# The sixth tile's attention visit moved ahead of its blocks, and five instead of three of its block pairs by seven products

## The chip, the cores and the metric

The kernel runs on one core of one Trainium2 chip. The metric is device time in microseconds (us) of one execution; less is better. The three runs of the kernel before have a median of 218.5 us (218.24 to 219.65).

## What is computed

A linear-attention recurrence with decay (retention) over 4 sequences of 768 steps, 8 heads of 64, and behind it a bilinear feed-forward layer on its 3072 output rows of 512:

```
for t in range(S):
    state = gamma * state + einsum('bhd,bhe->bhde', k[:, :, t], v[:, :, t])
    y[:, :, t] = scale * einsum('bhd,bhde->bhe', q[:, :, t], state)
x = y.transpose(0, 2, 1, 3).reshape(B * S, H * D)      # 3072 x 512
out = ((x @ w_a) * (x @ w_b)) @ w_out                  # 512 -> 1536 -> 512
```

Inputs and output are float32; the kernel multiplies in bfloat16.

## The kernel before

**Attention.** The rows are cut into 24 slots of 128 (6 a sequence). For two slots at a time a *visit*, the function `turn(new, old)`, issues a block of small 64x64 matmuls: for the old pair the part of its output that comes from the state, in two halves (L375), for the new pair the chunk states (st, L300) and the scores (at, L330), and for the old pair the part within the chunk (L387). Between the two halves of the state's part stands a fence: a tiny ACT copy `mark` (L352) waits for PE's first half, and PE's second half waits for `mark`. What follows a visit is done later by other engines: DVE adds the chunk states up (sums, L314) and masks the scores (aT, L336), ACT casts the states (gst, L207) and casts the finished outputs y into the feed-forward input xt (L402, `leave`). The ACT pieces wait in a list, `later`, from which `catch_up(n)` issues the next n; the masks wait in `unmasked`, from which `mask_now` issues them. POOL scales k and q (kqb, L248) and casts v (vb, L209); the transposes kqT are DMAs on SP's queue.

**Feed-forward.** The 24 slots make 8 tiles (J = 0 to 7) of 4, 2, 2, 2, 2, 4, 4 and 4 slots, so tiles 5, 6 and 7 have 512 rows. For each tile PE runs twelve a blocks (`ffn_a`, L614, four 128x512 matmuls) and twelve g blocks (`ffn_g`, L626), one for each 128 of the 1536 inner columns. ACT casts a to asb (L618) and DVE multiplies, ht = g * asb (L629). The output product ht @ w_out (`ffn_fast`, L786) is done by Winograd's form of Strassen's scheme: seven products instead of eight, with sums of ht (hsum, L684) as left and sums of w_out (wt_bf) as right operands. Its running sums stand in PSUM banks R1, R2 and R5: PE writes R1, ACT snaps it (snap, L798) or DVE adds a snap to it into the output tile osb (L801), and PE goes on writing to the same bank.

**Pairs by seven products.** In tiles 6 and 7 some pairs of a blocks are done in the same scheme (`seven_a`, L726: fourteen 128x256 matmuls instead of eight of 128x512). `SEVEN` gives the range of pairs f: 1 to 3 in tile 6, 1 to 5 in tile 7. The left operands are the weights wa_bf and sums of them, ta, which POOL makes (`combine_a(f)`, L704, four instructions a pair); the right ones are the tile's xt and sums of it, xs, which DVE makes (`combine_x(J)`, L695, four instructions). Their PSUM banks (`own_banks`) are those that a visit uses for y, at and st. ACT snaps them (L743, L746, L753, L765) and DVE adds them up (L740). The sums hsum of such pairs are made on POOL (`sums_of`), those of plain blocks on DVE.

**The order.** Each engine executes its instructions in the order in which the program issues them (`seq` chains them). The main loop runs the tiles one after the other, blocks and then output; a table `ahead` says what else is issued at which place: (6, 8) is ahead of block 8 of tile 6, (5, "late", 0) and (5, "sums", 0) are places in the first output product of tile 5, (6, "o", 0) is ahead of the output of tile 6. `gate` makes POOL's next instruction wait for DVE's last one. In tile 6 before: a(0), a(1), three pairs by seven products, the visit of slots 22 and 20, blocks 8 to 11 plain, the last visit (of 22 alone), the output.

Of the kernel before, what the change touches and what calls it, by code (L numbers as in the profile page):

```python
# [9 lines left out]
F32 = mybir.dt.float32  # L10
# [5 lines left out]
TILES = [4, 2, 2, 2, 2, 4, 4, 4]  # L16
FAST = (1, 2, 3, 4, 5, 6, 7)
ASIDE = ((1, 0), (2, 0), (3, 0), (4, 0), (5, 0), (6, 0), (6, 1), (7, 0))
SEVEN = {6: (1, 4), 7: (1, 6)}
SPARE = {(J, ft) for J in (2, 3, 4) for ft in range(1, 6 if J == 4 else 10, 2)}  # L20
PAIRS = 3

# [5 lines left out]
def kernel(  # L28
# [11 lines left out]
    P = 128  # L40
# [26 lines left out]
    psff = ctx.enter_context(tc.tile_pool(name="psff", bufs=3, space=bass.MemoryType.PSUM))  # L67
# [10 lines left out]
    def seq(bi):  # L78
        ins = bi.ins
        if gates and ins.engine == mybir.EngineType.Pool:  # L80
            tc.add_manual_dep(ins, gates.pop(), after, reason="behind VectorE's sums")
        prev = last.get(ins.engine)
        if prev is not None:
            tc.add_manual_dep(ins, prev.name, nosync, reason="program order")
        last[ins.engine] = ins
        return bi
# [101 lines left out]
    def late_tables():  # L188
        seq(nc.gpsimd.memset(mask, 1.0))
        for c in range(2):  # L190
            mc = mask[64 * c : 64 * c + 64]
            seq(nc.gpsimd.affine_select(out=mc, in_=mc, compare_op=ALU.is_ge, fill=0.0, base=0,
                                        pattern=[[0, 1], [1, 2], [2, D // 2]],
                                        channel_multiplier=-1))
        return positions([[P, NCH], [0, 1]], 1), positions([[P, NCH], [0, 1]], 2, True)

    late = late_tables()
# [32 lines left out]
    xt, where = {}, {}  # L230
# [48 lines left out]
    def catch_up(n=100):  # L279
        for fn in later[:n]:  # L280
            fn()
        del later[:n]
# [5 lines left out]
    sums = {}  # L288
# [103 lines left out]
    def new_xt(J):  # L392
        xt[J] = xtp.tile([P, 2, KT, 2, P], BF16, tag="xt", name="xt")

    def leave(o, c, apart):
        J, i = where[o]
        if i == 0 and c == 0:
            new_xt(J)
        dst = xt[J][:, i // 2].rearrange("p k par (s c m) -> p c s (k par) m", s=2, c=2)[:, c]
        src = ys[o][c].rearrange("p s k (par m) -> p s (k par) m", par=2)  # L400
        if apart is None:
            seq(nc.scalar.copy(dst, src))  # L402
        else:
            on, off = slice(4 - 4 * c, 8 - 4 * c), slice(4 * c, 4 * c + 4)
            part = tra.tile([P, 2, 2, D], F32, tag="kq"[c] + "T2", name="part", bufs=2)
            seq(nc.scalar.copy(part, apart[c][:, :, 2 - 2 * c : 4 - 2 * c]))
            part = part.rearrange("p s k (par m) -> p s (k par) m", par=2)
            for s in range(2):
                seq(nc.vector.tensor_tensor(dst[:, s, on], src[:, s, on], part[:, s], op=ALU.add))
                seq(nc.vector.tensor_copy(dst[:, s, off], src[:, s, off]))  # L410
# [161 lines left out]
    def xcols(J, kt, c0, c1):  # L572
        W2 = 2 * P
        x = xt[J][:, c0 // W2 : (c1 + W2 - 1) // W2, kt].rearrange("p u par m -> p u (par m)")
        return x if c1 - c0 > W2 else x[:, 0, c0 % W2 : c0 % W2 + c1 - c0]
# [18 lines left out]
    def parts(J, ft, c0, c1):  # L594

        if J == 0 and 2 <= ft < 10:
            return [(c0, (c0 + c1) // 2), ((c0 + c1) // 2, c1)]
        return [(c0, c1)]

    def ff_bank(J, ft, c, name):  # L600

        if (J, ft) in SPARE:
            return psat.tile([P, 4 * P], F32, tag=f"y{c}", name=name)
        return psff.tile([P, 4 * P], F32, tag="ff", name=name)

    def ffn_a(J, ft, c0=0, c1=None):
        c1 = TILES[J] * P if c1 is None else c1
        if J not in ht:
            ht[J] = htp.tile([P, NFT, 4 * P], BF16, tag="ht", name="ht")
        fs = slice(ft * P, (ft + 1) * P)  # L610
        a = ff_bank(J, ft, 0, "a")[:, : c1 - c0]
        for kt in range(KT):
            for b0, b1 in parts(J, ft, c0, c1):
                seq(nc.tensor.matmul(a[:, b0 - c0 : b1 - c0], wa_bf[:, kt, fs], xcols(J, kt, b0, b1),  # L614
                                     start=(kt == 0 and b0 == c0), stop=(kt == KT - 1 and b1 == c1),
                                     skip_group_check=True))
        asb = asbs[J, ft, c0] = asbp.tile([P, 4 * P], BF16, tag="asb", name="asb")[:, : c1 - c0]
        seq(nc.scalar.copy(asb, a))  # L618
# [69 lines left out]
    def combine_x(J):  # L688
        xs[J] = raw.tile([P, 4, 2, 2 * P], BF16, tag="q" * (J == 6) + "k" * (J == 7) + "f", name="xs")
        a11, a12, a21, a22 = (xt[J][:, u, 2 * c : 2 * c + 2].rearrange("p k par m -> p k (par m)")  # L690
                              for u in range(2) for c in range(2))
        s1, s2, s3, s4 = (xs[J][:, i] for i in range(4))
        for dst, x, y, op in ((s1, a21, a22, ALU.add), (s2, s1, a11, ALU.subtract),
                              (s4, a12, s2, ALU.subtract), (s3, a11, a21, ALU.subtract)):
            seq(nc.vector.tensor_tensor(dst, x, y, op=op))  # L695
# [12 lines left out]
    def own_banks(J):  # L708
        at = psat.tile([P, 2, 4 * P], F32, tag="at", name="a")
        st = psst.tile([P, 4 * P], F32, tag="st", name="a")  # L710
        y = [psat.tile([P, 4 * P], F32, tag=f"y{c}", name="a") for c in range(2)]
        banks[J] = [[y[f % 2][:, : 2 * P], st[:, : 2 * P], at[:, f % 2, : 2 * P]] for f in range(2)]
# [16 lines left out]
    def seven_a(J, f):  # L729

        W2 = 2 * P
        if J not in banks:
            own_banks(J)
        R1, R2, R5 = banks[J][f % 2]
        snap = raw.tile([P, 4, W2], F32, tag="vf", name="snap")
        even, odd = (asbp.tile([P, 4 * P], BF16, tag="asb", name="asb") for _ in range(2))
        asbs[J, 2 * f, 0], asbs[J, 2 * f + 1, 0] = even, odd

        def plus(dst, R, x):
            seq(nc.vector.tensor_tensor(dst, R, x, op=ALU.add))  # L740

        part_a(J, f, R1, 1, True)
        seq(nc.scalar.copy(snap[:, 0], R1))  # L743
        part_a(J, f, R2, 2, True)
        part_a(J, f, R5, 5, True)
        seq(nc.scalar.copy(snap[:, 2], R5))  # L746
        for fn in behind[:1]:
            fn()
        plus(even[:, :W2], R2, snap[:, 0])
        catch_up(2)  # L750
        ffn_g(J, 2 * f - 1)
        part_a(J, f, R1, 6, False)
        seq(nc.scalar.copy(snap[:, 1], R1))  # L753
        for fn in behind[1:]:
            fn()
        behind.clear()
        part_a(J, f, R5, 3, False)
        plus(odd[:, :W2], R5, snap[:, 1])
        catch_up(2)
        ffn_g(J, 2 * f - 2)  # L760
        part_a(J, f, R1, 7, False)

        def last_of():
            part_a(J, f, R1, 4, False)
            seq(nc.scalar.copy(even[:, W2:], R1))  # L765

        behind.extend((lambda: plus(odd[:, W2:], R1, snap[:, 2]), last_of))
# [145 lines left out]
    W2 = 2 * P  # L913
# [46 lines left out]
    for j in range(NO):  # L960
# [14 lines left out]
        (5, 0): [(casts, 20, "kq")], (5, 2): [(casts, 21, "kq"), (casts, 20, "v"), (casts, 21, "v")],  # L975
        (5, 3): [(turn, 16, None)], (5, 5): [(casts, 22, "kq")],
        (5, 6): [(casts, 23, "kq")], (5, 8): [(turn, 18, 16)],
        (5, "late", 0): [(gate,), (combine_a, 1), (casts, 22, "v"), (casts, 23, "v"), (combine_a, 2), (combine_a, 3)],
        (5, "sums", 0): [(turn, 20, 18)],
        (6, 8): [(turn, 22, 20)], (6, "o", 0): [(turn, None, 22)], (6, "late", 0): [(gate,), (combine_a, 4), (combine_a, 5)],  # L980
    }
    early = {3: [(0, 0, 2)], 4: [(1, 0, 2)], 5: [(2, 0, 2)], 6: [(3, 0, 2)],
             7: [(0, 2, 4)], 8: [(1, 2, 4)], 9: [(2, 2, 4)], 10: [(3, 2, 4)]}
# [4 lines left out]
    def visit(*at):  # L988
        for fn, *what in ahead.pop(at, ()):
            fn(*what)  # L990
# [8 lines left out]

    def blocks_seven(J):  # L1000
        f0, f1 = SEVEN[J]
        combine_x(J)
        store()
        for ft in range(2 * f0):
            ffn_a(J, ft)
        for f in range(f0, f1):
            seven_a(J, f)
            sums_of(J, f - 1)
            mask_now(1)
        seven_end(J, f1 - 1)  # L1010
        sums_of(J, f1 - 1)
        return 2 * f1
# [17 lines left out]
    def blocks(J):  # L1030
        done = blocks_seven(J) if J in SEVEN else 0
        for ft in range(done, NFT):
# [4 lines left out]
            if J in FAST:  # L1037
                for which, f0, f1 in adds_of(J, ft):
                    if J not in SEVEN or f0 >= 4:
                        add(J, which, f0, f1)  # L1040
# [3 lines left out]
    for J in range(len(TILES)):  # L1044
        if J > 1:
            blocks(J)
        for i in range(TILES[J]):
# [6 lines left out]
            elif i % 2 == 0:  # L1054
                if not J in SEVEN:
                    for which, f0, f1 in adds_of(J, NFT):
# [33 lines left out]
```

## Time and profile before

| | |
|---|---|
| median of three runs | 218.5 us (218.24 to 219.65) |
| the profiled execution | 218.93 us |
| its span on the core | 217.2 us |
| granted TensorE clock (mean) | 0.999 |
| DVE, busy share | 68% |
| POOL, busy share | 57% |
| ACT, busy share | 45% |

The span is what the trace shows; the execution's own time has 1.7 us around it. Times in rows are microseconds from the span's start. A timeline row gives start, duration, engine, line, operation, tiles written and read, shape and count, and in brackets how long the engine sat idle ahead of it and what released it. Line numbers are those of the kernel before.

### The profile page before, as it was taken

The page shows a single profiled execution, that of the slowest core. Times are in us where ns is not written, and L with a number is a line of the kernel's source. Part 1 is how long each engine was busy: PE and PEld are TensorE (multiplying, and loading weights), DVE is VectorE, ACT ScalarE, POOL GpSimd, SP SyncE. Part 2 cuts the span into 40 slices and gives each one's busy share as a digit, 9 for nine tenths or more (in the row PEclk, how much of TensorE's full clock was granted, in tenths as well). Part 3 has the DMA queues.
Part 4 walks back from the last instruction along what each step waited for, and adds up shares of the span by engine and source line. Part 5 has one row for each costly group of instructions (what it writes and reads, how often), then busy time and mean ns, then how long its engine had stood idle before and what let it go on. Part 6 is the DMA issues. An engine that isn't in the chain of part 4 may idle for free.

```text
span 217.2 us, 7074 instructions
## 1 busy us (share of the span) xinstructions
PE 210.6 (97%) x2877; PEld 156.0 (72%) x2877; DVE 148.4 (68%) x328; ACT 97.5 (45%) x243; POOL 124.1 (57%) x191
## 2 busy tenths in 40 slices
PE   8889999999999999999999999999999999999993
PEld 7568886686468888888887445478665488666682
DVE  2784456647767788797696387976877674777731
ACT  3775234442436436437465342736441642434231
POOL 6557789682553828482839264729429508087400
PEclk9999999999999999999999999999999999999999
DMA  5999999988999999899989899922200002200022
GB/s 169 347 376 382 372 301 395 363 193 133 243 220 207 246 291 207 193 277 202 195 201 261 186 274 214 214 65 98 98 0 3 3 0 100 98 0 5 0 97 97
DMA packets 94832, 39.77 MB, mean 183 GB/s; under 512 B 76112, under 2 KB 91728, under 8 KB 94800
## 3 DMA queue, kind: packets, MB, share of 16 engines
q1 hardware_dynamic: 94656, 39.20, 69.7%
q8 instruction: 22, 0.36, 0.6%
q10 hardware_dynamic: 144, 0.13, 0.2%
q14 instruction: 10, 0.08, 0.1%
HBM read 28.31 MB, written 6.29 MB: 159 GB/s over the span
## 4 chain that ended last, share of the span: by engine, by line
PE 83%; DMA 7%; DVE 4%; SPq 2%; POOL 1%; issue 1%; ACT 1%; DVEq 0%; POOLq 0%; ACTq 0%
PE g L626 28%; PE a L614 22%; PE o L786 21%; PE a L726 6%; DMA kf<-in_k_dram 3%; DMA vf<-in_v_dram 3%; DMA kqT<-kqb 2%; DVE ht L629 1%; PE y L375 1%; POOL kqb L245 1%; PE y L387 1%; PE at L330 1%; SPq L101 1%; PE st L300 1%; DVE wt_bf L225 1%
## 5 line engine op out<-in xcount | busy, mean ns | idle before, releaser
L629 DVE TENSOR_TENSOR ht<-g,asb 128x256 bf16<-128x256 f32 (+1 forms) x98 | 53.6, 548 | 36.6 <-PE g L626 28.8
L626 PE MATMUL g<-xt,wb_bf 128*128 128x256 bf16 (+1 forms) x424 | 77.9, 311 | 0.1
L614 PE MATMUL a<-xt,wa_bf 128*128 128x256 bf16 (+1 forms) x360 | 60.8, 299 | 0.1
L618 ACT CAST asb<-a 128x256 bf16<-128x256 f32 (+1 forms) x82 | 36.8, 450 | 50.4 <-PE a L614 49.2
L626 PEld LDWEIGHTS <-wb_bf 128*128 128x128 bf16 x424 | 41.3, 98 | 16.9 <-issue 0.3
L614 PEld LDWEIGHTS <-wa_bf 128*128 128x128 bf16 x360 | 34.6, 98 | 12.7 <-DVE xt L209 0.4
L248 POOL TENSOR_TENSOR kqb<-kf,ktab 128x256 bf16<-128x256 f32 x28 | 17.0, 627 | 24.9 <-DMA kf<-in_k_dram 22.1
L786 PEld LDWEIGHTS <-hsum 128*128 128x128 bf16 x240 | 23.2, 98 | 2.9
L798 ACT COPY snap<-o 128x256 f32<-128x256 f32 x38 | 14.2, 374 | 21.3 <-PE o L786 20.8
L786 PE MATMUL o<-wt_bf,hsum 128*128 128x256 bf16 x180 | 21.9, 273 | 0.0
L248 POOL TENSOR_TENSOR kqb<-qf,qtab 128x256 bf16<-128x256 f32 x28 | 17.6, 648 | 4.2 <-DMA qf<-in_q_dram 4.2
L209 POOL CAST vb<-vf 128x512 bf16<-128x512 f32 x30 | 17.8, 625 | 3.8 <-DMA vf<-in_v_dram 2.6
L786 PEld LDWEIGHTS <-ht 128*128 128x128 bf16 x180 | 17.2, 98 | 3.4 <-DVE ht L629 0.5
L684 POOL TENSOR_TENSOR hsum<-ht 128x256 bf16<-128x256 bf16 (+1 forms) x15 | 11.0, 734 | 15.0 <-DVE ht L629 8.1
L786 PE MATMUL o<-wo_bf,ht 128*128 128x256 bf16 x120 | 15.0, 273 | 0.0
L314 DVE TENSOR_TENSOR sums<-st,sums 128x256 f32<-128x256 f32 x30 | 12.7, 424 | 3.0 <-PE st L300 1.7
L704 POOL TENSOR_TENSOR ta<-wa_bf 128x256 bf16<-128x256 bf16 x10 | 6.9, 687 | 11.6 <-DVE osb L801 11.6
L801 DVE TENSOR_TENSOR osb<-o,snap 128x256 f32<-128x256 f32 x22 | 9.2, 418 | 6.1 <-PE o L786 3.3
L207 ACT CAST gst<-sums 128x256 bf16<-128x256 f32 x33 | 12.8, 409 | 0.5 <-DVE sums L312 0.3
L684 DVE TENSOR_TENSOR hsum<-ht 128x256 bf16<-128x256 bf16 (+2 forms) x33 | 12.8, 392 | 0.3
L245 POOL TENSOR_TENSOR kqb<-kf,ktab 128x512 bf16<-128x512 f32 x7 | 7.7, 1102 | 7.9 <-DMA kf<-in_k_dram 7.9
L336 DVE TENSOR_TENSOR aT<-at,mask 128x512 bf16<-128x512 f32 x18 | 12.2, 681 | 0.0
(100 smaller groups left out, 278.3 us busy)
## 6 DMA issues: line engine op xcount, KB each, us to landing
out_dram<-osb SPq DMA_DIRECT2D x11, 512.0 KB, 3.2
kf<-in_k_dram SPq DMA_DIRECT2D x18, 256.0 KB, 3.7
qf<-in_q_dram SPq DMA_DIRECT2D x36, 128.0 KB, 3.6
vf<-in_v_dram SPq DMA_DIRECT2D x18, 256.0 KB, 4.5
wsta<-in_moe_w_a_dram SPq DMA_DIRECT2D x6, 512.0 KB, 7.7
wstb<-in_moe_w_b_dram SPq DMA_DIRECT2D x6, 512.0 KB, 7.4
wsto<-in_moe_w_out_dram SPq DMA_DIRECT2D x6, 512.0 KB, 9.1
kf<-in_k_dram SPq DMA_DIRECT2D x3, 512.0 KB, 6.0
```

The source lines that it names most:

```text
L207: seq(nc.scalar.copy(dst, src))
L209: seq(engine.tensor_copy(dst, src))
L248: seq(eng.tensor_tensor(dst[:, r], src[:, r], tab[:, r], op=ALU.mult))
L314: seq(nc.vector.tensor_tensor(new, u[c][:, s], old, op=ALU.add))
L614: seq(nc.tensor.matmul(a[:, b0 - c0 : b1 - c0], wa_bf[:, kt, fs], xcols(J, kt, b0, b1), start=(kt == 0 and b0 == c0), stop=(kt == KT - 1 a ...
L618: seq(nc.scalar.copy(asb, a))
L626: seq(nc.tensor.matmul(g[:, b0 - c0 : b1 - c0], wb_bf[:, kt, fs], xcols(J, kt, b0, b1), start=(kt == 0 and b0 == c0), stop=(kt == KT - 1 a ...
L629: seq(nc.vector.tensor_tensor(ht[J][:, ft, c0:c1], g, asbs.pop((J, ft, c0)), op=ALU.mult))
L684: seq(eng.tensor_tensor(s[which], x(), y(), op=op))
L726: seq(nc.tensor.matmul(R, w, x, start=(first and k == 0), stop=(k == 1), skip_group_check=True))
L786: seq(nc.tensor.matmul(R[:, :DH], lhs, (wo_bf, wt_bf)[w][:, f, m, :], start=(first and f == 0), stop=(f == NH - 1), skip_group_check=True))
L798: seq(nc.scalar.copy(snap[:, i], R[:, :DH]))
```

## The change

The pairs by seven products in tile 6 become 1 to 5 instead of 1 to 3, so that blocks 8 to 11 are no longer plain. The visit of slots 22 and 20 goes from ahead of block 8 to behind a(0); directly behind it both leaves are issued (the second half first) and both masks. The first of these pairs takes its R5 from the general pool of banks. combine_x(6) goes from the start of tile 6 into the second output product of tile 5. All five combine_a stand together in tile 5's first output product, behind the two v casts; the two that stood in tile 6's output are gone from there. The hsum of pairs 4 and 5 are thereby made on POOL. `leave` makes a new xt whichever half comes first.

```diff
-SEVEN = {6: (1, 4), 7: (1, 6)}
+SEVEN = {6: (1, 6), 7: (1, 6)}
...
     def leave(o, c, apart):
         J, i = where[o]
-        if i == 0 and c == 0:
+        if J not in xt:
             new_xt(J)
...
         R1, R2, R5 = banks[J][f % 2]
+        if (J, f) == (6, 1):
+            R5 = psff.tile([P, 4 * P], F32, tag="ff", name="a")[:, :W2]
...
-        (5, "late", 0): [(gate,), (combine_a, 1), (casts, 22, "v"), (casts, 23, "v"), (combine_a, 2), (combine_a, 3)],
-        (5, "sums", 0): [(turn, 20, 18)],
-        (6, 8): [(turn, 22, 20)], (6, "o", 0): [(turn, None, 22)], (6, "late", 0): [(gate,), (combine_a, 4), (combine_a, 5)],
+        (5, "late", 0): [(gate,), (casts, 22, "v"), (casts, 23, "v")] + [(combine_a, f) for f in range(1, 6)],
+        (5, "sums", 0): [(turn, 20, 18)], (5, "sums", 1): [(combine_x, 6)],
+        (6, "a", 0): [(turn, 22, 20), (deal, 1, 0, 2, 3, 4), (catch_up, 2), (mask_now,)],
+        (6, "o", 0): [(turn, None, 22)],
...
     def blocks_seven(J):
         f0, f1 = SEVEN[J]
-        combine_x(J)
+        if J == 7:
+            combine_x(J)
         store()
         for ft in range(2 * f0):
             ffn_a(J, ft)
+            visit(J, "a", ft)
```

In the built program the lines behind the third edit stand two lower (L801 becomes L803). DVE at the end of tile 5's output and the start of tile 6, before:

```order
L336 TENSOR_TENSOR aT<-at,mask 128x512
L801 TENSOR_TENSOR osb<-o,snap 128x256 x3
L695 TENSOR_TENSOR xs<-xt 128x512
L695 TENSOR_TENSOR xs<-xs,xt 128x512
L695 TENSOR_TENSOR xs<-xt,xs 128x512
L740 TENSOR_TENSOR asb<-a,snap 128x256
L629 TENSOR_TENSOR ht<-g,asb 128x512
```

and now:

```order
L336 TENSOR_TENSOR aT<-at,mask 128x512
L803 TENSOR_TENSOR osb<-o,snap 128x256
L695 TENSOR_TENSOR xs<-xt 128x512
L695 TENSOR_TENSOR xs<-xs,xt 128x512
L695 TENSOR_TENSOR xs<-xt,xs 128x512
L803 TENSOR_TENSOR osb<-o,snap 128x256 x2
L314 TENSOR_TENSOR sums<-st,sums 128x256 x3
L336 TENSOR_TENSOR aT<-at,mask 128x512 x2
L742 TENSOR_TENSOR asb<-a,snap 128x256
L629 TENSOR_TENSOR ht<-g,asb 128x512
```

The xs instructions (a fourth, like the first, follows the third in both) moved past two osb sums; the first of these two reads R1, which PE's last product of tile 5 writes again. Sums and masks of the moved visit follow.

ACT from the last copy of tile 5's output to the first pair by seven products, before:

```order
L851 COPY osb<-o 128x256
L618 CAST asb<-a 128x512 x2
L743 COPY snap<-a 128x256
L746 COPY snap<-a 128x256
L753 COPY snap<-a 128x256
```

and now:

```order
L853 COPY osb<-o 128x256
L618 CAST asb<-a 128x512
L352 COPY mark<-bq 128x1
L402 CAST xt<-y 128x2x8x32 x2
L618 CAST asb<-a 128x512
L745 COPY snap<-a 128x256
L748 COPY snap<-a 128x256
L207 CAST gst_161<-sums 128x256
```

The fence's copy and the two leaves came between the casts of a(0) and a(1), and a state's cast behind the second snap.

POOL behind the scaling of slot 23, before:

```order
L704 TENSOR_TENSOR ta<-wa_bf,ta 128x2x128
L209 CAST vb<-vf 128x512 x2
L704 TENSOR_TENSOR ta<-wa_bf 128x2x128
L704 TENSOR_TENSOR ta<-wa_bf,ta 128x2x128
L684 TENSOR_TENSOR hsum<-ht 128x512
```

and now:

```order
L248 TENSOR_TENSOR kqb<-qf,qtab_745 128x4x64 x2
L209 CAST vb<-vf 128x512 x2
L704 TENSOR_TENSOR ta<-wa_bf 128x2x128
L704 TENSOR_TENSOR ta<-wa_bf,ta 128x2x128
L704 TENSOR_TENSOR ta<-wa_bf 128x2x128
L704 TENSOR_TENSOR ta<-wa_bf,ta 128x2x128
```

Before, four ta instructions stood ahead of the casts and eight behind them, then tile 6's sums; now the casts come first and all twenty ta instructions behind them, ahead of the sums, of which tile 6 has twenty instead of twelve.

## The prediction

> **What bounds the kernel now.** I read the page first (busy time, then the chain that ended last), then the timeline of PE around tile 6, and then those of DVE, POOL and ACT over the same microseconds, to see who would be waited for when an edit moves work.
>
> ```profile
> PE 210.6 (97%) x2877; PEld 156.0 (72%) x2877; DVE 148.4 (68%) x328; ACT 97.5 (45%) x243; POOL 124.1 (57%) x191
> PE 83%; DMA 7%; DVE 4%; SPq 2%; POOL 1%; issue 1%; ACT 1%; DVEq 0%; POOLq 0%; ACTq 0%
> ```
>
> PE is busy 97% of the span and 83% of the chain is PE's own work. So the change can win only the matmul time that it takes out, and it loses whatever PE waits for in its new order. PE around tile 6 (start, duration, line, tiles, count):
>
> ```profile
> 151.96 0.82 PE L786 MATMUL o<-wt_bf,ht 128*128 128x256 bf16 x6
> 152.61 1.89 PE L614 MATMUL a<-xt,wa_bf 128*128 128x512 bf16 x8
> 154.34 0.60 PE L726 MATMUL a<-xt,wa_bf 128*128 128x256 bf16 x4
> 155.86 0.38 PE L726 MATMUL a<-xs,ta 128*128 128x256 bf16 x2
> 157.38 0.60 PE L726 MATMUL a<-xt,wa_bf 128*128 128x256 bf16 x4
> 160.63 0.60 PE L726 MATMUL a<-xt,wa_bf 128*128 128x256 bf16 x4
> 166.19 0.32 PE L375 MATMUL y<-kqT,gst 64*64 64x64 bf16 x16
> 166.84 0.32 PE L375 MATMUL y<-kqT,gst 64*64 64x64 bf16 x16
> 167.38 1.04 PE L614 MATMUL a<-xt,wa_bf 128*128 128x512 bf16 x4
> 174.39 0.32 PE L375 MATMUL apart<-kqT,gst 64*64 64x64 bf16 x16
> 175.03 1.49 PE L786 MATMUL o<-wo_bf,ht 128*128 128x256 bf16 x12
> 177.01 2.13 PE L786 MATMUL o<-wt_bf,hsum 128*128 128x256 bf16 x18
> ```
>
> Durations overlap (matmuls are pipelined), so I use differences of starts. 151.96 is the last product of tile 5's output; 152.61 the blocks a(0) and a(1), 0.87 each; 154.34 to 166.19 the three pairs by seven products and their end; 166.19 to 167.38 the visit of slots 22 and 20 (1.19); 167.38 to 174.39 four a and four g blocks in the plain way; 174.39 the last visit, 175.03 the output.
>
> **The change part by part.**
>
> *Pairs 4 and 5 by seven products.* One steady pair slot goes from 157.38 to 160.63, 3.25, g blocks included. Two of them are 6.50. They replace the plain stretch of 7.01 (167.38 to 174.39). Gain 0.51. A gain beyond that has no source: PE's timeline from 152 to 184 carries no idle time in any row.
>
> *combine_x(6) moves to the middle of tile 5's last output.* This puts four DVE instructions ahead of the osb sum that reads R1, and the product that PE starts at 151.96 writes R1 again, so it waits for that sum. Before, the sum was ready just in time. DVE, then POOL:
>
> ```profile
> 149.69 0.41 DVE L801 TENSOR_TENSOR osb<-o,snap 128x256 f32<-128x256 f32 x1
> 151.48 0.42 DVE L801 TENSOR_TENSOR osb<-o,snap 128x256 f32<-128x256 f32 x1 [1.38 <-PE o L786]
> 152.41 0.77 DVE L695 TENSOR_TENSOR xs<-xt 128x512 bf16<-128x512 bf16 x1
> 153.21 0.77 DVE L695 TENSOR_TENSOR xs<-xs,xt 128x512 bf16<-128x512 bf16 x1
> 154.02 0.77 DVE L695 TENSOR_TENSOR xs<-xt,xs 128x512 bf16<-128x512 bf16 x1
> 154.72 0.41 DVE L695 TENSOR_TENSOR xs<-xt 128x512 bf16<-128x512 bf16 x1
> 166.36 0.69 DVE L629 TENSOR_TENSOR ht<-g,asb 128x512 bf16<-128x512 f32 x1 [0.61 <-PE g L626]
> 184.77 0.41 DVE L695 TENSOR_TENSOR xs<-xt 128x512 bf16<-128x512 bf16 x1
> ```
>
> ```profile
> 145.11 0.67 POOL L704 TENSOR_TENSOR ta<-wa_bf 128x256 bf16<-128x256 bf16 x1 [4.12 <-DVE osb L801]
> 148.86 0.67 POOL L704 TENSOR_TENSOR ta<-wa_bf 128x256 bf16<-128x256 bf16 x1
> 149.61 0.67 POOL L704 TENSOR_TENSOR ta<-wa_bf,ta 128x256 bf16<-128x256 bf16 x1
> 150.24 0.67 POOL L704 TENSOR_TENSOR ta<-wa_bf 128x256 bf16<-128x256 bf16 x1
> 152.23 0.67 POOL L704 TENSOR_TENSOR ta<-wa_bf,ta 128x256 bf16<-128x256 bf16 x1
> 152.86 0.85 POOL L704 TENSOR_TENSOR ta<-wa_bf 128x256 bf16<-128x256 bf16 x1
> 153.67 0.85 POOL L704 TENSOR_TENSOR ta<-wa_bf,ta 128x256 bf16<-128x256 bf16 x1
> 161.46 1.15 POOL L684 TENSOR_TENSOR hsum<-ht 128x512 bf16<-128x512 bf16 x1 [6.94 <-ACT snap L743]
> 166.01 0.67 POOL L684 TENSOR_TENSOR hsum<-ht 128x256 bf16<-128x256 bf16 x1
> 168.65 0.67 POOL L684 TENSOR_TENSOR hsum<-ht 128x256 bf16<-128x256 bf16 x1
> ```
>
> The three xs instructions beside POOL's ta work took 0.77 each, the POOL instructions beside them 0.85; the fourth xs, with POOL at rest, and the first of tile 7 took 0.41. So here the two engines hinder each other, and in the new place POOL is in the ta work throughout: it starts at 145.11 as before, the two vb casts and the first four ta exchange places within the same 3.75, so POOL reaches 148.86 at the same phase, and twenty ta instead of twelve keep it busy to about 160.
> The working: DVE is free at about 150.05, with a POOL instruction (149.61) in progress. At 152.41 the like case ended 0.32 behind the start of the next POOL instruction (152.41 + 0.77 = 153.18 against 152.86), so the first xs ends at 150.24 + 0.32 = 150.56. The second and third follow by the 0.81 of the rows (151.37, 152.18), the fourth ends 0.70 to 0.81 later, at about 152.95. The osb sum starts some 0.07 before that end, as DVE rows overlap, and is done near 153.30; PE follows 0.06 after (151.48 + 0.42 = 151.90 against 151.96), at 153.35 instead of 151.96. Loss 1.39. Bounds: four at 0.41 give a loss of 0.24; four that each sit out a whole POOL instruction give 2.45 (rivals one and two). I take the rows of the same four instructions on the same tile beside the same POOL work.
> The rule that speaks against this change: the Trainium skill, page "SBUF — State Buffer", section "SBUF: two separate sides", says that a DVE instruction with two SBUF inputs and a GpSimd instruction that reads SBUF take one port pair by an exclusive lock for the whole instruction. The trace agrees in kind (0.77 against 0.41), but not in full, since 0.41 + 0.67 would be 1.08 an instruction against 0.81; taken to the letter it is rival two.
> Behind the late sum on DVE stand R5's osb sum, the sums and the masks of the visit. PE needs them only after a(0), so they add nothing of their own.
>
> *The visit of slots 22 and 20 moves from behind the pairs to behind a(0).* Its matmuls are the same. Its vb casts and transposes are long done, it issues no DMA, and SP's order is unchanged. But the fence: a small ACT copy (mark) must follow PE's first 16 matmuls and precede the second 16, and ACT now has a(0)'s cast in front of it.
>
> ```profile
> 152.81 0.37 ACT L851 COPY osb<-o 128x256 f32<-128x256 f32 x1 [1.68 <-PE o L786]
> 153.73 0.58 ACT L618 CAST asb<-a 128x512 bf16<-128x512 f32 x1 [0.55 <-PE a L614]
> 155.08 0.38 ACT L743 COPY snap<-a 128x256 f32<-128x256 f32 x1
> 166.56 0.19 ACT L352 COPY mark<-bq 128x1 f32<-128x1 f32 x1 [0.76 <-PE y L375]
> 168.45 0.58 ACT L618 CAST asb<-a 128x512 bf16<-128x512 f32 x1 [1.70 <-PE a L614]
> 168.93 1.08 ACT L402 CAST xt<-y 128x512 bf16<-128x512 f32 x2
> ```
>
> Before, ACT was idle at the fence (0.76) and mark was done at 166.75, before PE came to it at 166.84. After: a(0) starts at 153.35 + 0.65 = 154.00, its cast 1.12 later (153.73 - 152.61) at 155.12, mark 0.48 behind (168.93 - 168.45) at 155.60, done 155.79, PE goes on at 155.85. PE arrives at 154.87 + 0.65 = 155.52. Loss 0.33; bounds 0 (the cast starts earlier) and 0.6 (the whole cast is in the way).
>
> Then the two leaves stand on ACT ahead of a(1)'s cast and of the snap that frees R1 for 155.86's matmul. PE ends the visit at 154.87 + 1.19 + 0.33 = 156.39; a reader follows some 0.20 later (152.81 against 151.96 + 0.65), so the leaves run 156.59 to 157.67 (1.08 for two) and a(1)'s cast, which could start at 157.51, is 0.16 late. The snap ended at 155.46 with 0.40 to spare, so 0.24 is left. R1 itself waits for the first leave, free at 157.2, as PE arrives at 157.25. I count nothing; at worst 0.2.
>
> *Sums of pairs 4 and 5 go from DVE to POOL.* The first pair now starts 157.25 - 154.34 = 2.91 later, so POOL's 161.46 becomes 164.37. Four long sums (4.55 to 166.01), then 2.64 a pair (166.01 to 168.65): pairs 2, 3 and 4 end at 171.56, 174.20, 176.84, and pair 5, whose last ht comes at 174.39 + 1.21 + 0.17 + 0.69 = 176.46, follows at once; its second sum ends at 176.84 + 0.75 + 0.67 = 178.26. PE asks for it at the sixth matmul of the hsum product: 175.60 + 0.64 + 1.98 + 0.55 = 178.77. Cover: the last visit and three products; 0.5 to spare, so nothing. The late combine_a of tiles 4 and 5 are done by 160, and their removal from tile 6's output frees an engine that no one waited for there.
>
> **Sum:** -0.51 + 1.39 + 0.33 = +1.21. The profiled execution took 218.93 (span 217.2), 0.43 over the median of 218.5; 218.93 becomes 220.14, the median 219.7, 0.55% slower.
>
> **The rivals.**
> *One: DVE and POOL do not collide in the new place; not slower.* The xs run at 0.41 as at 184.77, done by 150.05 + 1.64 = 151.69; the sum is ready at 152.14, PE at 152.20, loss 0.24. Sum -0.51 + 0.24 + 0.33 = +0.06: 218.6; with the fence hidden too, 218.2. For it: DVE wins some meetings. Against: three of three in the rows lost 0.36, and POOL's rows stand back to back.
> *Two: each xs sits out a whole POOL instruction; slower by over 1%.* First xs 149.61 + 0.67 + 0.41 = 150.69, three more at 1.08: 153.93; sum 154.35, PE 154.41, loss 2.45. Total +2.27: 220.8. It makes over 1% once the spacing is over 1.05. Another place bears it out nearly:
>
> ```profile
> 61.13 1.32 POOL L245 TENSOR_TENSOR kqb<-qf,qtab 128x512 bf16<-128x512 f32 x1 [2.21 <-DMA qf<-in_q_dram]
> 61.46 1.40 DVE L684 TENSOR_TENSOR hsum<-ht,hsum 128x768 bf16<-128x768 bf16 x1
> ```
>
> There DVE ended 0.41 behind the POOL instruction. Against it: the 0.81 spacing of the very same pair of loops. This is the page's lock taken to the letter.
> *Three: POOL's tail becomes the bound.* If its sums run at the 0.81 spacing of 152.86 to 153.67 instead of 0.66, sixteen of them end 2.4 later, 1.9 past the slack: +3.1, 221.6. Against: DVE there reads PSUM in every instruction, and 166.01 to 168.65 kept 0.66 beside such work. It decides past 0.5 of delay.
>
> **How the numbers follow.** Forecast 219.7 with 0.60 (its own range 219.3 to 220.2, the loss of 1.39 by 0.2 and the fence by 0.3 either way); rival one 0.18, two 0.12, three 0.06, anything else 0.04. A measurement of this kernel, whose three runs span 0.6%, tells about 1% from no change. Over 1% faster (below 216.3) has no mechanism, 0.02; over 1% slower (above 220.7) takes three, the half of two that lies beyond it and a little besides, 0.13; the rest, 0.85, lies within. To hold 8 in 10 the range takes in rival one's lower end and rival two: 218.2 to 220.9.
>
> **What would show it.** Right: on DVE four xs at 0.5 to 0.8 directly behind the third-last osb of tile 5, the next osb with PE waiting for it 1.2 to 1.6; a wait of PE of about 0.3 inside the visit with mark directly behind a(0)'s cast; five pair slots of 3.25; no wait at tile 6's hsum products; everything from there on 1.2 later than before. Wrong: xs at 0.41 or over 1.0, no wait ahead of tile 6, pair slots over 3.3 or PE waiting for POOL's hsum.

## The result and the profile after

The changed kernel has a median of 220.01 us over 22 runs against 218.95 for the kernel before over 22 runs taken with it. The ratio is 1.0055, 95% interval 1.0037 to 1.0072: slower by 0.55%, about 1.2 us. The forecast was 219.7 against a median of 218.5, 0.55% as well. The profiled execution took 219.66 with a span of 218.0.

The stages of the two profiled executions, one row each: length, then busy time of PE, PEld, DVE, ACT and POOL with the number of their instructions, then granted clock, DMA share and GB/s. In both the cuts are the start of the hsum products in tile 5's second output, of its last product, of the first pair by seven products, and of the last visit. Of the kernel before:

```profile
149.25:151.96 2.71, 2.71 (x26) 2.34 (x24) 1.28 (x3) 1.85 (x6) 2.63 (x5) 1.00 0.50 197
151.96:154.34 2.38, 2.38 (x15) 1.37 (x14) 2.20 (x4) 0.96 (x2) 2.30 (x4) 1.00 0.14 55
154.34:174.39 20.05, 19.95 (x228) 11.32 (x226) 14.26 (x28) 9.09 (x23) 9.80 (x13) 1.00 0.06 22
174.39:217.20 42.81, 39.26 (x359) 29.25 (x358) 25.75 (x63) 14.53 (x40) 16.83 (x26) 1.00 0.13 50
```

and of the changed kernel:

```profile
148.77:152.87 4.10, 2.78 (x26) 2.35 (x24) 4.03 (x8) 1.86 (x6) 3.94 (x6) 1.00 0.34 132
152.87:156.75 3.88, 3.81 (x134) 2.46 (x134) 1.87 (x5) 1.78 (x5) 3.80 (x7) 1.00 0.35 139
156.75:175.11 18.36, 18.26 (x119) 11.43 (x118) 13.92 (x28) 8.55 (x25) 13.62 (x20) 1.00 0.00 1
175.11:218.00 42.89, 39.26 (x359) 29.27 (x358) 24.31 (x56) 14.50 (x40) 15.49 (x24) 1.00 0.13 50
```

The first stage is 1.39 longer with the same 26 matmuls: PE is busy for 2.78 of 4.10, DVE for 4.03, nearly all of it. The second holds the moved visit and is 1.50 longer, the third no longer holds it and is 1.69 shorter; together they give 0.19 back. The last is the same within 0.1. The changed execution reached the first cut 0.48 earlier (148.77 against 149.25). POOL was as much ahead when it began the first moved instruction (144.62 against 145.11), so this is no effect of the change; it is why the two spans differ by 0.8 and not by 1.2.

PE at these places in the changed kernel (in brackets the idle time ahead of a row and what ended it):

```profile
150.73 0.82 PE L788 MATMUL o<-wo_bf,hsum 128*128 128x256 bf16 x6
152.87 0.81 PE L788 MATMUL o<-wt_bf,ht 128*128 128x256 bf16 x6 [1.32 <-DVE osb L803]
153.52 1.03 PE L614 MATMUL a<-xt,wa_bf 128*128 128x512 bf16 x4
154.48 0.32 PE L375 MATMUL y<-kqT,gst 64*64 64x64 bf16 x16
155.37 0.32 PE L375 MATMUL y<-kqT,gst 64*64 64x64 bf16 x16
155.88 1.04 PE L614 MATMUL a<-xt,wa_bf 128*128 128x512 bf16 x4
156.75 0.60 PE L726 MATMUL a<-xt,wa_bf 128*128 128x256 bf16 x4
159.79 0.60 PE L726 MATMUL a<-xt,wa_bf 128*128 128x256 bf16 x4
163.05 0.60 PE L726 MATMUL a<-xt,wa_bf 128*128 128x256 bf16 x4
175.11 0.32 PE L375 MATMUL apart<-kqT,gst 64*64 64x64 bf16 x16
```

Tile 5's last product waited 1.32 for DVE's osb sum. Inside the visit the second half starts 0.89 behind the first, not 0.65. Pair 2 takes 3.26 (159.79 to 163.05). ACT at the fence:

```profile
154.64 0.59 ACT L618 CAST asb<-a 128x512 bf16<-128x512 f32 x1 [0.55 <-PE a L614]
155.12 0.19 ACT L352 COPY mark<-bq 128x1 f32<-128x1 f32 x1
156.97 0.60 ACT L618 CAST asb<-a 128x512 bf16<-128x512 f32 x1
```

The mark stands directly behind a(0)'s cast and is done at 155.31; PE goes on at 155.37. The last row is a(1)'s cast: it starts 1.09 behind a(1), a(0)'s 1.12 behind a(0), so the two leaves between them did not hold it up. DVE and POOL beside the wait for the osb sum:

```profile
149.21 0.41 DVE L803 TENSOR_TENSOR osb<-o,snap 128x256 f32<-128x256 f32 x1
149.54 0.52 DVE L695 TENSOR_TENSOR xs<-xt 128x512 bf16<-128x512 bf16 x1
150.10 0.77 DVE L695 TENSOR_TENSOR xs<-xs,xt 128x512 bf16<-128x512 bf16 x1
150.91 0.78 DVE L695 TENSOR_TENSOR xs<-xt,xs 128x512 bf16<-128x512 bf16 x1
151.60 0.88 DVE L695 TENSOR_TENSOR xs<-xt 128x512 bf16<-128x512 bf16 x1
152.41 0.74 DVE L803 TENSOR_TENSOR osb<-o,snap 128x256 f32<-128x256 f32 x2
```

```profile
149.12 0.67 POOL L704 TENSOR_TENSOR ta<-wa_bf,ta 128x256 bf16<-128x256 bf16 x1
149.74 0.85 POOL L704 TENSOR_TENSOR ta<-wa_bf 128x256 bf16<-128x256 bf16 x1
150.55 0.85 POOL L704 TENSOR_TENSOR ta<-wa_bf,ta 128x256 bf16<-128x256 bf16 x1
177.06 0.67 POOL L684 TENSOR_TENSOR hsum<-hsum,ht 128x256 bf16<-128x256 bf16 x1
```

The four xs take turns with POOL: their ends lie 0.79 to 0.82 apart, and the osb sum starts 2.87 behind the start of the first of them. The last row answers for POOL's tail: pair 5's second sum ended at 177.73, and PE asked for it behind the last visit (0.64), three products (1.98) and five matmuls (0.55): 175.11 + 0.64 + 1.98 + 0.55 = 178.28.

### The profile page after: what moved, and what is told of

Same layout as the page of the kernel before. It is cut to its first block, busy times and chain, and to the rows that moved or that the text cites. A ratio compares the mean times of both kernels' runs of the same rounds, so it can differ in the third digit from the quotient of the medians.

```text
span 218.0 us, 7107 instructions
## 1 busy us (share of the span) xinstructions
PE 209.2 (96%) x2886; PEld 157.0 (72%) x2889; DVE 147.5 (68%) x326; ACT 97.7 (45%) x247; POOL 129.5 (59%) x199
## 4 chain that ended last, share of the span: by engine, by line
PE 90%; DMA 3%; DVE 2%; POOL 1%; ACT 1%; issue 1%; SPq 0%; POOLq 0%; DVEq 0%
PE g L626 28%; PE o L788 22%; PE a L614 21%; PE a L726 7%; PE o L661 5%; DMA kf<-in_k_dram 3%; PE y L375 2%; POOL kqb L245 1%; PE y L387 1%; PE at L330 1%; PE st L300 1%; DVE ht L629 1%; PE y L545 1%; PE tp L466 1%; PE st L507 1%
## 5 line engine op out<-in xcount | busy, mean ns | idle before, releaser
L614 PE MATMUL a<-xt,wa_bf 128*128 128x256 bf16 (+1 forms) x344 | 56.9, 295 | 0.1
L618 ACT CAST asb<-a 128x256 bf16<-128x256 f32 (+1 forms) x78 | 34.5, 443 | 47.6 <-PE a L614 46.3
L614 PEld LDWEIGHTS <-wa_bf 128*128 128x128 bf16 x344 | 33.0, 98 | 10.9 <-DVE xt L209 0.4
L248 POOL TENSOR_TENSOR kqb<-kf,ktab 128x256 bf16<-128x256 f32 x28 | 17.5, 644 | 26.0 <-DMA kf<-in_k_dram 18.2
L684 POOL TENSOR_TENSOR hsum<-ht 128x256 bf16<-128x256 bf16 (+1 forms) x19 | 13.7, 719 | 18.2 <-DVE ht L629 18.2
L803 DVE TENSOR_TENSOR osb<-o,snap 128x256 f32<-128x256 f32 x22 | 9.1, 416 | 5.6 <-ACT snap L800 3.7
L742 DVE TENSOR_TENSOR asb<-a,snap 128x256 bf16<-128x256 f32 x30 | 11.9, 418 | 1.1 <-ACT snap L745 0.9
L726 PEld LDWEIGHTS <-ta 128*128 128x128 bf16 x80 | 7.8, 98 | 6.1 <-issue 0.8
```

What stands on the lines that cost most here:

```text
L248: seq(eng.tensor_tensor(dst[:, r], src[:, r], tab[:, r], op=ALU.mult))
L684: seq(eng.tensor_tensor(s[which], x(), y(), op=op))
L726: seq(nc.tensor.matmul(R, w, x, start=(first and k == 0), stop=(k == 1), skip_group_check=True))
```

## The experiments

Theory: the time is a sum of three terms on PE, the wait for the osb sum behind the xs (dear because POOL works beside them), the wait at the fence behind a(0)'s cast, and the gain of two more pairs. The rivals put the loss elsewhere: into the moved visit, into DVE's queue as such, or into POOL's tail. Each ratio below is to the kernel before, run alongside, with its 95% interval; each profile is of one execution.

**The move of the xs alone**, in the kernel before.

```diff
-        combine_x(J)
+        if J == 7:
+            combine_x(J)
...
-        (5, "sums", 0): [(turn, 20, 18)],
+        (5, "sums", 0): [(turn, 20, 18)], (5, "sums", 1): [(combine_x, 6)],
```

> The kernel before with one part of the change alone: combine_x(6) stands in the middle of tile 5's last output product. POOL's order is that of before, so ta work runs there too. Theory (the xs instructions share time with POOL's ta at about 0.8 us each and hold up the osb sum that frees R1): PE waits about 1.4 us ahead of tile 5's last product, nothing is won, the total is 1.4 us over before (ratio 1.006). Rival, the loss belongs to the moved visit or to the longer ta work and not to the place of the xs: the wait is at most 0.3 us and the total within 0.3 us of before (ratio 1.001). Rival, part of the loss is given back because DVE has the xs behind it when tile 6 begins: 0.5 to 1.0 us over.

Ratio 1.0052, interval 1.0021 to 1.0084. PE's row in its profile:

```profile
154.96 0.81 PE L786 MATMUL o<-wt_bf,ht 128*128 128x256 bf16 x6 [1.22 <-DVE osb L801]
```

The hsum products there begin at 150.96, so the first stage is 4.00, 1.29 over the kernel before. Nothing is given back in tile 6: its pairs and blocks take 20.05, as before. This one move carries the whole net loss of the change.

**POOL at rest beside the xs**, in the changed kernel: the ta of pairs 2 to 5 wait for DVE's xs.

```diff
-        (5, "late", 0): [(gate,), (casts, 22, "v"), (casts, 23, "v")] + [(combine_a, f) for f in range(1, 6)],
-        (5, "sums", 0): [(turn, 20, 18)], (5, "sums", 1): [(combine_x, 6)],
+        (5, "late", 0): [(gate,), (casts, 22, "v"), (casts, 23, "v"), (combine_a, 1)],
+        (5, "sums", 0): [(turn, 20, 18)], (5, "sums", 1): [(combine_x, 6), (gate,)] + [(combine_a, f) for f in range(2, 6)],
```

> The changed kernel, with combine_a of pairs 2 to 5 held back until DVE has done combine_x(6), so that POOL is at rest beside the xs. Theory (the collision with POOL makes the xs dear): each xs takes 0.41 to 0.43 us, PE's wait ahead of tile 5's last product shrinks from 1.39 to about 0.25 us, and the total falls by 1.1 us, to about before (ratio 1.000). Rival, the xs are dear by themselves in that place (their place in DVE's queue alone costs the wait): they stay near 0.77 us and the total at ratio 1.0055. Rival, POOL then ends its sums too late at tile 6's end: the xs are cheap but PE waits for hsum, some 1 us, and the total stays near ratio 1.005; by the rows POOL would end ta near 161.5 us, ahead of the first sums at about 162.7, so I expect no such wait.

Ratio 0.9992, interval 0.9967 to 1.0017. DVE's first and last xs, POOL's next instruction and PE's last product of tile 5:

```profile
150.05 0.41 DVE L695 TENSOR_TENSOR xs<-xt 128x512 bf16<-128x512 bf16 x1
151.30 0.42 DVE L695 TENSOR_TENSOR xs<-xt 128x512 bf16<-128x512 bf16 x1
```

```profile
151.80 0.67 POOL L704 TENSOR_TENSOR ta<-wa_bf 128x256 bf16<-128x256 bf16 x1 [2.01 <-DVE xs L695]
```

```profile
152.11 0.82 PE L788 MATMUL o<-wt_bf,ht 128*128 128x256 bf16 x6
```

With POOL idle for 2.01 the same four instructions in the same place cost 0.18 of PE's time (152.11 - 149.22 = 2.89 against 2.71). The place in the queue is cheap; the collision costs the other 1.2. POOL's ta ended at 162.35 and its first sum started at 163.10: no tail.

**POOL busy without reading.** To see what in POOL's work collides, its ta of pairs 2 and 3 were replaced by memsets. This kernel leaves those sums out, so only its times are of use.

```diff
         for dst, x, y in ((t1, b12, b11), (t2, b22, t1), (t3, b22, b12), (t4, b21, t2)):
-            seq(nc.gpsimd.tensor_tensor(dst, x, y, op=ALU.subtract))
+            if f in (2, 3):
+                for _ in range(3):
+                    seq(nc.gpsimd.memset(dst, 0.0))
+            else:
+                seq(nc.gpsimd.tensor_tensor(dst, x, y, op=ALU.subtract))
```

> The changed kernel, in which POOL fills the ta of pairs 2 and 3 with zeros, twelve memsets a pair, instead of computing them (these pairs' products are left wrong, so the time alone is of use). POOL is then busy beside the xs, but with instructions that read nothing. Theory, the collision is one over reading SBUF, as the Trainium skill's page SBUF: State Buffer says of DVE instructions with two SBUF inputs (its section on SBUF's two separate sides: only against a GpSimd instruction that reads SBUF): xs at 0.41 to 0.43 us, wait of PE ahead of tile 5's last product 0.2 us. Rival, any busy POOL instruction holds the xs up: xs at 0.5 us and more, wait 0.5 to 1.4 us, since a memset is shorter than a ta instruction.

It ran once, at 218.91 against 218.19 for the kernel before, also run once; two single runs do not settle the total, so the rows have to. POOL and DVE:

```profile
148.88 7.98 POOL L706 MEMSET ta<- 128x256 bf16 x24
```

```profile
150.05 0.41 DVE L695 TENSOR_TENSOR xs<-xt 128x512 bf16<-128x512 bf16 x1
150.50 0.43 DVE L695 TENSOR_TENSOR xs<-xs,xt 128x512 bf16<-128x512 bf16 x1
```

POOL wrote without a pause from 148.88 to 156.86 and the xs ran as if alone; the first stage was 2.83, 0.12 over before. So a busy POOL is not enough for the collision; what the memsets leave out is the sums' reading of SBUF. (A memset row is also shorter, 0.33 against 0.67.) The Trainium skill, page "SBUF — State Buffer", section "Who interferes with whom", says this: a DVE instruction with two SBUF inputs contends with a GpSimd instruction that reads SBUF, not with one that only writes it. The trace agrees (0.43 beside memsets, 0.77 beside ta).

**The fence on DVE.**

```diff
-        (6, "a", 0): [(turn, 22, 20), (deal, 1, 0, 2, 3, 4), (catch_up, 2), (mask_now,)],
+        (6, "a", 0): [(turn, 22, 20, nc.vector), (deal, 1, 0, 2, 3, 4), (catch_up, 2), (mask_now,)],
```

> The changed kernel, with the fence of the moved visit copied by DVE instead of ACT. DVE has been idle there for 1.9 us. Theory (PE loses 0.33 us because the fence stands behind a(0)'s cast on ACT): the second half of the visit's matmuls starts 0.65 us behind the first half instead of 0.89, and the total falls by 0.25 to 0.35 us (ratio to before about 1.004). Rival, the wait inside the visit is only moved, because PE then waits for the first leave or a(1)'s cast: the visit is shorter by 0.25 us but the first pair starts no sooner, total unchanged (1.0055).

Ratio 1.0039, interval 1.0011 to 1.0067. The two halves of the visit on PE:

```profile
155.21 0.32 PE L375 MATMUL y<-kqT,gst 64*64 64x64 bf16 x16
155.85 0.32 PE L375 MATMUL y<-kqT,gst 64*64 64x64 bf16 x16
```

0.64 apart: the wait in the visit is gone, and a(0) to a(1) takes 2.15 instead of 2.36, so 0.21 was the fence's, less than the 0.25 to 0.35 expected. The interval overlaps that of the changed kernel, and the profiled execution does not settle the total either: its first xs took 0.63 instead of 0.52, and the first stage, ahead of the edit, 4.27 instead of 4.10.

**Three pairs again**, all else as changed.

```diff
-SEVEN = {6: (1, 6), 7: (1, 6)}
+SEVEN = {6: (1, 4), 7: (1, 6)}
```

> The changed kernel with three pairs by seven products in tile 6 as before; blocks 8 to 11 are plain again and their sums are on DVE, the visit and the xs stay in their new places. Theory (two more pairs are worth 0.51 us of PE's time): 0.4 to 0.5 us over the changed kernel, ratio to before about 1.008. Rival, the two pairs win nothing, since their gain is lost in waits on ACT and DVE: same as the changed kernel, 1.0055. Rival, POOL's longer tail of sums costs more than the pairs win: below the changed kernel.

Ratio 1.006, interval 1.0033 to 1.0086; by itself that does not part it from 1.0055. The profile does: from pair 3 to the last visit

```profile
163.77 0.60 PE L726 MATMUL a<-xt,wa_bf 128*128 128x256 bf16 x4
176.23 0.32 PE L375 MATMUL apart<-kqT,gst 64*64 64x64 bf16 x16
```

it takes 12.46, and the changed kernel 12.06 (163.05 to 175.11) from the same pair to the same visit. Two more pairs are worth 0.40, not 0.51.

**The xs in two halves**: two stay, two go behind tile 5's last sums (`combine_x` takes as its second argument which of the four to issue).

```diff
-        (5, "sums", 0): [(turn, 20, 18)], (5, "sums", 1): [(combine_x, 6)],
+        (5, "sums", 0): [(turn, 20, 18)], (5, "sums", 1): [(combine_x, 6, slice(0, 2))],
...
-        if J == 7:
-            combine_x(J)
+        combine_x(J, slice(2 if J == 6 else 0, 4))
```

> The changed kernel with the four xs instructions split: the first two stay in the middle of tile 5's last output product, the other two stand at tile 6's start, behind the osb sums. POOL's order is unchanged, so they still collide. Theory (PE's loss is the delay of the osb sum, and two xs at 0.5 and 0.77 us are over before that sum's PSUM is ready): no wait of over 0.1 us ahead of tile 5's last product, the later two hidden behind a(0), the total 1.39 us below the changed kernel, 0.2 us below before (ratio 0.999). Rival, the later two xs hold up the visit's sums on DVE and PE waits for the st bank at the first pair: up to 0.5 us comes back (ratio 1.001). Rival, the cost of the xs does not come from the osb sum: ratio stays near 1.005.

Ratio 0.9995, interval 0.9977 to 1.0013. DVE and PE:

```profile
149.85 0.41 DVE L696 TENSOR_TENSOR xs<-xt 128x512 bf16<-128x512 bf16 x1
150.30 0.78 DVE L696 TENSOR_TENSOR xs<-xs,xt 128x512 bf16<-128x512 bf16 x1
151.31 0.42 DVE L804 TENSOR_TENSOR osb<-o,snap 128x256 f32<-128x256 f32 x1 [0.24 <-PE o L789]
152.24 0.90 DVE L696 TENSOR_TENSOR xs<-xt,xs 128x512 bf16<-128x512 bf16 x1
```

```profile
151.79 0.81 PE L789 MATMUL o<-wt_bf,ht 128*128 128x256 bf16 x6
```

The first xs got through at 0.41, and the second and third still collide (0.78, 0.90). But DVE is now idle 0.24 waiting for PE ahead of the osb sum, and the first stage is 2.71 as before. Here the collision cost PE nothing, because nothing that PE waited for stood behind it.

**Both cures together**, the split and the fence on DVE (the edits of both runs).

> The split of the xs and the fence on DVE together. Theory (the three terms add up): minus 0.51, with no other loss, so 0.4 to 0.5 us below before, ratio 0.998. Rival, with the fence on DVE the mark now stands behind the two later xs and is late: the loss of 0.3 us in the visit stays or grows to 0.8 (ratio 0.9995 to 1.002).

Ratio 0.9985, interval 0.9967 to 1.0002. The mark and the visit:

```profile
155.29 0.14 DVE L352 COPY mark<-bq 128x1 f32<-128x1 f32 x1
```

```profile
154.83 0.32 PE L375 MATMUL y<-kqT,gst 64*64 64x64 bf16 x16
155.49 0.32 PE L375 MATMUL y<-kqT,gst 64*64 64x64 bf16 x16
```

PE goes on 0.06 behind the mark and 0.66 behind the visit's start, where 0.65 were due, so the xs ahead of the mark cost it nothing. The changed stretch is 0.40 shorter than in the kernel before (24.74 against 25.14). This version is clearly faster than the changed kernel; over the kernel before its interval just reaches 1, so that part rests on the profile.

**The xs back at tile 6's start**, all else as changed.

```diff
-        if J == 7:
-            combine_x(J)
+        combine_x(J)
...
-        (5, "sums", 0): [(turn, 20, 18)], (5, "sums", 1): [(combine_x, 6)],
+        (5, "sums", 0): [(turn, 20, 18)],
```

> The changed kernel with all four xs at the start of tile 6, where the kernel before had them. Theory: no wait ahead of tile 5's last product; the xs collide with POOL's ta and end some 3 us later, so the visit's sums on DVE start late and PE waits about 0.3 us for the st bank at the first pair; total about 1.1 us below the changed kernel, 0.1 us over before (ratio 1.0005). Rival, DVE's delay is carried through the pairs, each of which waits for DVE's adds: 1 us or more comes back (ratio 1.004 to 1.006), so that the place chosen by the change costs nothing on balance.

Ratio 1.0012, interval 0.9998 to 1.0026. The second bank of pair 1, and the sums that it waits for:

```profile
155.96 0.38 PE L726 MATMUL a<-xt,wa_bf 128*128 128x256 bf16 x2 [0.22 <-DVE sums L314]
```

```profile
155.04 1.33 DVE L314 TENSOR_TENSOR sums<-st,sums 128x256 f32<-128x256 f32 x3
```

Pair 1 took 3.45 (155.35 to 158.80) instead of 3.04, so the late sums cost 0.41; the pairs behind it took 3.25 each. The place that the change chose avoids this 0.41 and pays 1.39 for it.

The same stretch in every profile, from the hsum products of tile 5's second output to the last visit, worked out from PE's rows. The stretch also holds tile 5's last product (about 0.65) and block a(1) (about 0.87), which are nearly the same in every row:

| kernel | first stage | a(0) to a(1) | pairs and blocks | stretch | over before |
|---|---|---|---|---|---|
| before | 2.71 | 0.87 | 20.05 (with the visit) | 25.14 | |
| changed | 4.10 | 2.36 | 18.36 | 26.34 | +1.20 |
| move of xs alone | 4.00 | 0.87 | 20.05 (with the visit) | 26.43 | +1.29 |
| POOL at rest | 2.89 | 2.36 | 18.36 | 25.13 | -0.01 |
| POOL on memsets | 2.83 | 2.36 | 18.36 | 25.07 | -0.07 |
| fence on DVE | 4.27 | 2.15 | 18.36 | 26.30 | +1.16 |
| three pairs | 4.08 | 2.35 | 18.75 | 26.71 | +1.57 |
| xs split | 2.71 | 2.36 | 18.36 | 24.95 | -0.19 |
| split, fence on DVE | 2.71 | 2.15 | 18.35 | 24.74 | -0.40 |
| xs back | 2.71 | 2.36 | 18.77 | 25.36 | +0.22 |

## Why the prediction was right, point by point

- *The wait for the osb sum.* Forecast 1.39, measured 1.39 (4.10 - 2.71), by the mechanism named: put there by the move alone, taken away by POOL's rest or by the split. Set 0.48 later, to the clock of the trace before, the first xs ended at 150.54 (forecast 150.56) and the osb sum started at 152.89 (forecast 152.88). To the hundredth it is luck: where the first xs took 0.42, 0.49, 0.52 and 0.63 (the move alone, three pairs, the changed kernel, the fence on DVE), the wait was 1.29, 1.37, 1.39 and 1.56, all within the 0.2 either way that the forecast allowed. The fourth xs took 0.88, but started 0.69 behind the third.
- *The gain of two pairs.* Forecast 0.51, mis-sized: 0.40. The other 0.1 of the replaced stretch was the step into a visit. A block ahead of a visit lasts 0.96 to the next start (153.52 to 154.48) and one ahead of another block 0.87. The visit took that 0.09 along to its new place, where the forecast left it out (154.00 to 154.87).
- *The fence.* Forecast 0.33, mis-sized: PE waited 0.24 (0.89 - 0.65), and without the wait the visit was 0.21 shorter. The second half started 1.85 behind a(0) (153.52 to 155.37), as forecast (154.00 to 155.85); but the step into the visit let PE arrive 0.09 later, so it waited that much less. Both mis-sizings come from this one step and have opposite signs, which is why the sum held: -0.40 + 0.21 + 1.39 = 1.20 against the forecast 1.21 and 1.20 in the trace. The stretches themselves were right (a(0) to a(1) forecast 2.39, measured 2.36; pairs and blocks 20.05 - 1.19 - 0.51 = 18.35 against 18.36); it was their division into causes that was off.
- *What was counted at nothing.* The leaves ahead of a(1)'s cast, the visit's masks and sums on DVE, and pair 5's sums on POOL delayed PE nowhere: PE's rows from a(1) on carry no idle time. POOL's tail had 178.28 - 177.73 = 0.55 to spare (forecast 0.5).
- *The rivals.* One (no collision) is what the run with POOL at rest shows: its cheap xs cost 0.18 (forecast 0.24), but the changed kernel collides. Two (the whole instruction sat out, 1.08 a turn) fell: the turns are 0.81. Three did not occur.

## What to carry to other kernels

Before an instruction goes into an engine's queue ahead of something that PE waits for, price it with what runs beside it in the new place, not in the old: four vector instructions of 0.42 us cost PE 0.18 with GpSimd at rest and 1.39 with GpSimd reading SBUF. Look first for the idle time already there: two of the four fitted into it free of charge, and the rest behind the sum. And when an edit worth 0.4 us comes with moves, each move needs its own line in the sum; here one of them took back over three times the gain.

## What the runs showed of the hardware

- The collision is not the sum of the two durations: a DVE instruction of 0.41 and a POOL instruction of 0.67 took turns at 0.81, so 0.27 of the two rows ran side by side. The forecast had read this spacing off the profile before, and it held in the new place. Where the first xs met a ta that began with it, POOL paid: in the split, 0.41 for the xs (149.85) and 0.91 for the ta (149.89). Where the ta was well under way, the xs paid too: 0.52 in the changed kernel (149.54, the ta from 149.12).
- POOL's memsets (0.33 each, back to back) did not disturb DVE at all.
- Going over from 128x128 matmuls to the 64x64 ones of a visit cost PE 0.09 each time: at three places in each of the two profiles the visit starts 0.95 or 0.96 behind the start of the 128x512 block ahead of it, where another block starts after 0.86 or 0.87. The Trainium skill, page "TensorEngine Tiling (Array Packing)", section "Key Properties", says that changing the tiling mode drains the engine. The 0.09 on the way in is in line with that, but no run here separates a drain from other costs of the step.
